# One v buffer, values in a register-addressed PE loop: attention decode on one Trainium2 core

## The chip, the cores and the metric

One core of a Trainium2 chip (trn2). The metric is the device time of one execution in microseconds (us), median of several executions. The engines: PE multiplies matrices, DVE is the vector engine, ACT the scalar engine; SyncE (SP) issues the loads, which sixteen DMA engines carry out. A load has landed when its last part is reported complete. PE's sequencer (`PEq`) is the part of PE that runs the program and hands instructions on.

## The reference

```python
B, H, Sq, Skv, Dh = 8, 32, 1, 4096, 128          # bfloat16
scores = jnp.einsum('bhqd,bhkd->bhqk', q, k) * Dh ** -0.5
attn = jax.nn.softmax(scores, axis=-1)
return jnp.einsum('bhqk,bhkd->bhqd', attn, v)
```

There are 256 heads with one query row each. k and v are 268 MB each and are read once. The kernel takes 8 heads per tile: 32 tiles, each with 8.39 MB of k and 8.39 MB of v.

## The kernel before: the parts that matter

Per tile: DVE multiplies k with the broadcast query row and folds the product (`product`), PE sums over the head dimension by matmuls with the identity (`sum_over_d`), DVE reduces to scores (`scores_of`), ACT takes exponentials (`weights_of`), and one tile later PE multiplies the weights with v (`values_of`). There are two k buffers and **one v buffer**: the next v load can be issued only when PE has read the last one.

```python
KB, VB = 2, 1
...
def load(kind, t):
    ...
        nc.sync.dma_start(buf[:, c0 : c0 + n, :], src[t, :, c0 : c0 + n, :])
...
def values_of(t, lo, hi):                      # 64 matmuls, four column groups
    ...
    for c0 in range(lo, hi, CB):
        i = c0 // CB
        j = group[i]                           # i % 4 for tiles 0 to 30
        nc.tensor.matmul(
            avs[t][j * AG : (j + 1) * AG, :], lhsT=w[:, i, :, :],
            rhs=vt[:, c0 : c0 + CB, :], start=(i < TG), stop=(j not in group[i + 1 :]),
        )
...
for t in range(NT):
    load("k", t + 1); load("v", t)             # (guards cut)
    product(t, 0, Q);  sum_over_d(t, 0)
    if t > 2 and t % R == 1:
        recip_of(n); finish_of(n)              # every eighth tile: writes 16 KB of output
    q_prep(t + 1)
    product(t, Q, 2 * Q);  sum_over_d(t, 1);  scores_of(t, 0)
    values_of(t - 1, 0, C);  copy_of(t - 1)    # (the last two tiles differ)
    product(t, 2 * Q, 3 * Q);  sum_over_d(t, 2);  scores_of(t, 1)
    product(t, 3 * Q, C);  sum_over_d(t, 3);  scores_of(t, 2)
    scores_of(t, 3);  weights_of(t)
    ...
```

## Time and profile before

| | before |
|---|---|
| median (range), us | 1253.25 (1252.86 to 1253.62) |
| span of the profiled run | 1252.0 us |
| data queue (q1), share of sixteen DMA engines | 99.3% = 1243.2 us per engine |
| DVE / PE busy | 1038.0 / 503.5 us |
| v landing to next v issue (mean of 29 tiles) | 6.1 us |

The first three rows say that the loads are the bound. A k load of 19.35 us runs while PE works on v, and the DMA queue's own waits show this (columns: us in total, times, longest):

```profile
SPq L138 <- DMA vt<-in_v_dram: 706.1, 30, 28.0
...
SPq L138 <- PE av L261: 176.2, 29, 10.6
```

For the 29 v loads SyncE waited for PE's values for at most 10.6 us, while DMA engines had a k load to do.

### The profile page before, as it was taken

How to read it: one execution, taken by the hardware profiler on the slowest of the kernel's cores; microseconds unless marked ns; L12 is line 12 of the kernel's file. 1: busy time of each engine (PE TensorE's matmuls, PEld its weight loads, DVE VectorE, ACT ScalarE, POOL GpSimd, SP SyncE). 2: the span in 40 equal slices, each digit the busy share in tenths (PEclk: the TensorE clock that was granted, in tenths of full speed). 3: DMA queues.
4: the chain of work that ended last, by engine and by line, in shares of the span. 5: the costliest groups of instructions: out<-in, count | busy, mean ns of one | idle time of the engine just before them, and what ended most of it. 6: DMA issues, size and time to landing. Idle time of an engine off the chain costs nothing.

```text
span 1252.0 us, 7714 instructions
## 1 busy us (share of the span) xinstructions
PE 503.5 (40%) x3067; PEld 175.8 (14%) x3067; DVE 1038.0 (83%) x588; ACT 172.6 (14%) x625; POOL 3.3 (0%) x18
## 2 busy tenths in 40 slices
PE   1334442444333453334443244432444324445355
PEld 0111110111111111111111111110111101111122
DVE  5988898888988889788898888987879888898991
ACT  0111011111011110111101111011110111101111
POOL 0000000000000000000000000000000000000000
PEclk9766656666556666566665566655666566665767
DMA  9999999999999999999999999999999999999997
GB/s 404 436 434 434 436 434 436 432 436 432 434 437 430 431 432 432 436 432 434 432 432 432 436 436 434 434 425 430 433 430 434 432 432 436 432 430 431 427 448 308
DMA packets 11444, 537.50 MB, mean 429 GB/s; under 512 B 1808, under 2 KB 2064, under 8 KB 2320
## 3 DMA queue, kind: packets, MB, share of 16 engines
q1 hardware_dynamic: 11072, 536.94, 99.3%
q8 instruction: 24, 0.39, 0.1%
q10 hardware_dynamic: 336, 0.07, 0.0%
q14 instruction: 12, 0.10, 0.0%
HBM read 536.94 MB, written 0.07 MB: 429 GB/s over the span
## 4 chain that ended last, share of the span: by engine, by line
DMA 75%; PE 15%; DVE 8%; issue 1%; ACT 0%; SPq 0%
DMA vt<-in_v_dram 74%; PE av L261 14%; DVE kt L171 5%; DVE kt L174 2%; PE ps L191 1%; DMA q_all<-in_q_dram 1%; DVE kt L179 0%; DVE sc L203 0%; DVE pmax L213 0%; SPq L138 0%; DVE spread L215 0%; DVE nmax L220 0%; ACT comb L288 0%; PE op L303 0%; ACT stage L312 0%
## 5 line engine op out<-in xcount | busy, mean ns | idle before, releaser
L171 DVE TENSOR_TENSOR kt<-kt,qb 128x8192 bf16<-128x8192 bf16 x128 | 565.2, 4415 | 92.4 <-DMA kt<-in_k_dram 80.8
L191 PE MATMUL ps<-kt,ident 128*128 128x512 bf16 x792 | 292.2, 527 | 663.5 <-DVE kt L179 508.5
L174 DVE TENSOR_TENSOR kt<-kt 128x4096 bf16<-128x4096 bf16 x128 | 293.4, 2292 | 4.4
L191 PEld LDWEIGHTS <-ident 128*128 128x128 bf16 x792 | 91.9, 119 | 824.7 <-issue 669.3
L261 PE MATMUL av<-vt,w 128*32 128x512 bf16 x2047 | 183.5, 529 | 52.0 <-DMA vt<-in_v_dram 52.0
L233 ACT ACTIVATE w<-sc,bias 128x256 bf16<-128x256 f32 x256 | 126.3, 494 | 357.8 <-DVE bias L224 357.8
L203 DVE TENSOR_REDUCE sc<-ps 128x64 f32<-128x512 f32 x128 | 87.8, 686 | 84.2 <-PE ps L191 84.2
L261 PEld LDWEIGHTS <-w 128*32 128x32 bf16 x2047 | 67.8, 127 | 178.9 <-issue 86.8
L288 ACT ACTIVATE comb<-av 128x512 bf16<-128x512 f32 x32 | 19.1, 596 | 424.7 <-PE av L261 424.7
L179 DVE TENSOR_TENSOR kt<-kt 128x2048 bf16<-128x2048 bf16 x58 | 71.0, 1225 | 2.0
L233 ACT ACTIVATION_READ_ACCUMULATOR w<-sc,bias 128x1 f32 x256 | 47.7, 186 | 0.0
L154 ACT ACTIVATE qg<-qh 8x128 bf16<-8x128 f32 x32 | 8.6, 267 | 186.9 <-PE qh L150 186.9
L312 ACT ACTIVATE stage<-op,rz 16x128 bf16<-16x128 f32 x16 | 5.7, 358 | 96.0 <-DVE rz L281 72.9
L303 PE MATMUL op<-comb,pick 128*16 128x128 bf16 x128 | 15.9, 265 | 4.6 <-ACT comb L288 4.6
L213 DVE TENSOR_REDUCE pmax<-sc 128x1 f32<-128x256 f32 x32 | 13.4, 420 | 1.1
L150 PE MATMUL qh<-q_all,ident 128*8 128x128 bf16 x32 | 8.5, 267 | 13.2 <-DMA q_all<-in_q_dram 13.2
L281 DVE RECIPROCAL rz<-zp 16x1 f32<-16x1 f32 x16 | 2.4, 148 | 13.3 <-PE zp L273 13.3
L156 PE MATMUL qp<-qg,heads 8*128 8x128 bf16 x32 | 8.3, 259 | 12.7 <-ACT qg L154 12.7
L303 PEld LDWEIGHTS <-pick 128*16 128x16 bf16 x128 | 9.0, 102 | 15.9 <-issue 15.8
L158 ACT ACTIVATE qb<-qp 128x128 bf16<-128x128 f32 x32 | 8.9, 278 | 11.1 <-PE qp L156 11.1
L215 DVE TENSOR_SCALAR spread<-same,pmax 128x32 f32<-128x32 f32 x32 | 7.7, 242 | 1.1
L224 DVE TENSOR_SCALAR bias<-own,nmax 128x8 f32<-128x8 f32 x32 | 7.4, 231 | 1.1
(25 smaller groups left out, 24.3 us busy)
## 6 DMA issues: line engine op xcount, KB each, us to landing
kt<-in_k_dram SPq DMA_DIRECT2D x7, 4096.0 KB, 35.3
kt<-in_k_dram SPq DMA_DIRECT2D x2, 2048.0 KB, 36.4
vt<-in_v_dram SPq DMA_DIRECT2D x1, 4096.0 KB, 40.7
vt<-in_v_dram SPq DMA_DIRECT2D x1, 2048.0 KB, 45.2
vt<-in_v_dram SPq DMA_DIRECT2D x1, 1024.0 KB, 47.2
vt<-in_v_dram SPq DMA_DIRECT2D x1, 512.0 KB, 48.0
vt<-in_v_dram SPq DMA_DIRECT2D x31, 32.9
kt<-in_k_dram SPq DMA_DIRECT2D x28, 43.7
```

Of the source, the lines that this page charges most:

```text
L154: nc.scalar.activation(out=qg[:], in_=qh[:], func=ACT.Copy)
L158: nc.scalar.activation(out=qb[:, 0, :], in_=qp[:], func=ACT.Copy)
L171: nc.vector.tensor_tensor(out=part, in0=part, in1=qb[:].to_broadcast([P, MC, D]), op=ALU.mult)
L174: nc.vector.tensor_tensor(out=part[:, :, 0 : D // 2], in0=part[:, :, 0 : D // 2], in1=part[:, :, D // 2 : D], op=ALU.add,)
L179: nc.vector.tensor_tensor(out=part[:, :, 0 : D // 4], in0=part[:, :, 0 : D // 4], in1=part[:, :, D // 4 : D // 2], op=ALU.add,)
L191: nc.tensor.matmul(ps[:], lhsT=ident[:], rhs=kt[:, u * UC : (u + 1) * UC, s * DS : (s + 1) * DS], start=(s == 0), stop=(s == n - 1),)
L203: nc.vector.tensor_reduce(out=scs[t][:, u * UC : (u + 1) * UC], in_=sums.pop((t, u))[:], axis=AX.X, op=ALU.add)
L213: nc.vector.tensor_reduce(out=pmax[:], in_=sc[:], axis=AX.X, op=ALU.max)
L233: nc.scalar.activation(out=w[:, :, g, :], in_=sc_g, func=ACT.Exp, bias=bias[:, g : g + 1], scale=scale, accum_out=esum[:, t % R, g : g + 1],)
L261: nc.tensor.matmul(avs[t][j * AG : (j + 1) * AG, :], lhsT=w[:, i, :, :], rhs=vt[:, c0 : c0 + CB, :], start=(i < TG), stop=(j not in group[ ...
L288: nc.scalar.activation(out=comb[:], in_=av, func=ACT.Copy)
L303: nc.tensor.matmul(ops[n][:], lhsT=pick[:, m, r, :], rhs=comb[:, m, :], start=(r == 0 and m == 0), stop=(r == R - 1 and m == CB - 1),)
```

## The change

The intent is to shorten PE's program (a loop in place of 64 unrolled matmuls per tile) and to keep DVE from waiting for PE, by putting the last two score quarters behind the next tile's first product. The loop's matmuls take their operands' addresses from registers, and all 64 matmuls of a tile go into one column group of PE (32 of its 128 columns) in place of four. `tc.tile_critical()` makes a region of the loop. Cut to its core:

```diff
-    sc_pool = ... bufs=1
+    sc_pool = ... bufs=2
+def values_loop(t):
+    ...
+    av = avs[t][0:AG, :]                       # one column group
+    with tc.tile_critical() as loop:
+        for i in range(EDGE): one(i, start=(i == 0), stop=False)        # EDGE = 2
+        end = (NV - EDGE) * nw
+        pe.reg_mov(rw, EDGE * nw); pe.reg_mov(rv, EDGE * nv)
+        with pe.While(lambda: pe.snap(rw, ...) < end):
+            ow = pe.snap(rw, ...); ov = pe.snap(rv, ...)
+            for i in range(LOOP):                                       # LOOP = 6
+                pe.matmul(av, lhsT=wf[:, bass.ds(ow + i * nw, nw)],
+                          rhs=vf[:, bass.ds(ov + i * nv, nv)], start=False, stop=False)
+            pe.reg_add(rw, rw, LOOP * nw); pe.reg_add(rv, rv, LOOP * nv)
+        for i in range(NV - EDGE, NV): one(i, start=False, stop=(i == NV - 1))
@@ order of a tile with a loop (0 < t <= NT - 3)
+            q_prep(t + 1)
             product(t, 0, Q)
             sum_over_d(t, 0)
+            scores_of(t - 1, 2); scores_of(t - 1, 3); weights_of(t - 1)
             if t > 2 and t % R == 1: recip_of(n); finish_of(n)
             product(t, Q, 2 * Q)
             sum_over_d(t, 1)
             scores_of(t, 0)
-            values_of(t - 1, 0, C)
+            values_loop(t - 1)
+            load("k", t + 1); load("v", t)     # were at the top of the tile
             copy_of(t - 1)
```

## The prediction

> **What bounds the kernel now.** I read, in this order, the page's slices, its table of DMA queues, the chain that ended last, the waits of the DMA queue, and a timeline of one tile in the middle.
>
> ```profile
> DMA  9999999999999999999999999999999999999997
> GB/s 404 436 434 434 436 434 436 432 436 432 434 437 430 431 432 432 436 432 434 432 432 432 436 436 434 434 425 430 433 430 434 432 432 436 432 430 431 427 448 308
> ...
> q1 hardware_dynamic: 11072, 536.94, 99.3%
> q8 instruction: 24, 0.39, 0.1%
> ...
> L191 PE MATMUL ps<-kt,ident 128*128 128x512 bf16 x792 | 292.2, 527 | 663.5 <-DVE kt L179 508.5
> ...
> L261 PE MATMUL av<-vt,w 128*32 128x512 bf16 x2047 | 183.5, 529 | 52.0 <-DMA vt<-in_v_dram 52.0
> ```
>
> The data queue holds the sixteen DMA engines for 99.3% of 1252.0 us, which is 1243.3 us per engine. The first packet starts at 1.76 us and the last one ends at 1246.8 us by the packet records, so nothing is left between; 5.2 us of tail follow. DVE is busy 1038.0 us, 32.4 per tile, and PE 503.5 us, 15.7 per tile: neither binds. The load of one tile (8.39 MB of k or of v) takes 8.39 MB / 434 GB/s = 19.35 us, the pair 38.7 us, and 32 pairs are 1238 us. This is the bound, and no work on PE makes it shorter. The skill's page "DMA: Bandwidth & Descriptors", section "Where 436 GB/s comes from", works out 435.2 GB/s as the ceiling of the sixteen ports; the slices lie at 430 to 437.
>
> The timeline of one tile, cut to what matters, shows what this hangs on:
>
> ```profile
> 67.89 4.23 PE L261 MATMUL av<-vt,w 128*32 128x512 bf16 x64
> ...
> 606.44 6.29 PE L261 MATMUL av<-vt,w 128*32 128x512 bf16 x64 [1.41 <-DMA vt<-in_v_dram]
> ...
> 612.78 0.33 SPq L138 DMA_DIRECT2D vt<-in_v_dram  x1
> ...
> 620.34 0.33 SPq L138 DMA_DIRECT2D kt<-in_k_dram  x1
> ...
> 625.85 4.42 DVE L171 TENSOR_TENSOR kt<-kt,qb 128x8192 bf16<-128x8192 bf16 x1 [3.56 <-DMA kt<-in_k_dram]
> ```
>
> There is one v buffer. A v tile lands at 606.4; PE multiplies it in 6.29 us; only then is the next v issued (612.78), while the k tile of that gap runs until 625.8. So the values may last longer at no cost until the v issue comes too late for the end of the k load. The k issue at 620.34 has the whole v load ahead of it and is far from late.
>
> **What the Trainium skill says.** "TensorE: Matmul & The Clock Gate", section "Wait — 56ns, not 53.3ns?", gives start to start 426.7 ns for 512 columns while the array is cold and 215.7 once warm; its Part 1 has a cold start last about 3.4 us of sustained work, in free-running windows. The trace agrees: four matmuls of four column groups start together, the next four 427 ns later, or 216 ns later once warm; the 64 take 4.23 to 6.5 us depending on when the clock rises (16 x 0.216 = 3.5 if all were warm). "TensorEngine Tiling", section "Available Configurations", has four independent tiles of 128x32; the 183.5 us of L261 over 2047 matmuls are 90 ns each, so they do run four abreast. "Advanced Engine Details and Errata", section "Control Flow Timing": an unconditional branch about 51 ns, compare-and-branch about 108. No run here has shown a loop yet. The warm bursts in this trace issue four weight loads and matmuls per 216 ns, so a fixed-address pair costs the sequencer 54 ns at most; for register addresses neither a page nor the trace has a cost.
>
> **The change, part by part.**
> *Values in one column group.* The 64 matmuls of tiles 0 to 28 (29 tiles) go one after another. Cold they cost 0.427 us each, warm 0.216. Before, the cold part lasted (from 16 x 0.216 + 0.211 n = 5.15 to 6.5, n = 8 to 14 groups) some 3.4 to 6 us. Now the loop follows the sums of the second quarter almost without a gap, so part of that is spent before it: I take 4 us. 4 / 0.427 = 9 cold ones, then 55 x 0.216 = 11.9: about 15.9 us, from 15.2 to 17. This adds 10 us of PE time per tile: (15.9 - 5.73) x 29 = 295 us of busy time, to some 800 us, and it lies beside the loads if the window holds it.
>
> *The loop's sequencer work.* Ten rounds of six matmuls, with two fixed ones at each end. In the built program each looped matmul has one fused register instruction ahead of it, each round one more, a register move, a compare-and-branch and a branch. My estimate from the skill's figures: 159 ns of branches per round; for the eight register instructions I assume 60 ns each, as for the slow decode of a matmul (about 62 ns, the same section of the clock gate page): 480; the six pairs with register addresses at twice 62 if they leave the fast path: 744. Sum 1383 ns per round, 231 per matmul; at 54 ns per pair it would be 161. Against 216 in the array the first is just about equal, and the cold start gives the sequencer a lead. So the array sets the 15.9 us, unless the register instructions cost much more than assumed. This is the step that I know least.
>
> *The window.* A v tile's data end about 0.5 us before its landing (last packet about 605.9, landing 606.4), and the first packet starts 1.0 us after the issue (0.74 to 1.76 at the start of the kernel). After a v landing the k load runs 19.35 us, so the issue may come 19.35 - 0.5 - 1.0 = 17.8 us after the landing. From this goes the entry. DVE starts tile t at its k landing; two quarters took 15.84 us (625.85 to 641.69), now with the two late score reductions and the four small steps between them (2.4 us): 18.3. The sums of the second quarter follow (4 x 0.427 = 1.8 and the latency of 0.2), so PE is free at 20.3, about 1.0 us after the v landing at 19.25. The waits and the branch into the loop I put at 0.4, the drain and the semaphore at its end at 0.25. Left for the loop: 17.8 - 1.0 - 0.4 - 0.25 = 16.1 us. The mean loop fits with 0.2 to spare, a cold one misses by up to 0.9. With lengths evenly between 15.2 and 17 the mean overrun is 0.2 us, 29 x 0.2 = 6 us on the path. A late v shifts all that follows, but the next entry then waits less for the sums.
>
> *Scores behind the next product.* DVE does the same work in another order (128 reductions of 0.68 us). This keeps DVE from waiting for sums of quarters 2 and 3, which PE now does after the loop, at about 37 us into the tile; DVE wants them at 38.7 + 8. Weights come at 10.5 + 4.0 (eight exponentials of 0.49) = 14.5 us into the next tile, 4.8 before the v landing. Hidden.
>
> *Fewer instruction fetches.* PE's rows fall from 6088 to 3014. The 24 fetches of 16 KB hold an engine 1.06 us each;[...] the completion records show the slowest of the sixteen 5 us behind the fastest at the end. Some nine fetches fewer are 9 x 1.06 / 16 = 0.6 us on average, on the slowest engine perhaps 1 to 1.5. Gain about 1.5.
>
> Sum: 1253.25 + 6 - 1.5 = 1257.8.
>
> **The rivals.**
> *The loop fits wholly.* If the sequencer is quick and the clock rises early, only the fetches count: 1251 to 1252. For it: 16 us is near the mean loop; the change looks sized for the window.
> *The sequencer binds.* At 300 ns per matmul the loop is 9 x 0.427 of lead and then the sequencer: 64 x 0.3 = 19.2 less what was fetched ahead, about 18.8 us. Then the v loads set the period: 19.35 + 1.5 + 0.65 + 18.8 = 40.3 instead of 38.7, 29 x 1.6 = 46 us: 1300. At 350 ns (21.8 us) the period is 43.3 and the time 1386. Nothing in the trace speaks against it.
> *The clock stays low* with a quarter of the array's columns at work: 64 x 0.427 = 27.3 us, period 48.8, 29 x 10.1 = 293 us: about 1545. Against it:[...] unlikely.
> *A gain over 2%* would need the bytes to move faster than 434 GB/s; the packets of 64 KB take 2.42 us each throughout. I see no way.
>
> **Range and chances.** The central number is 1258, barely over what the loads need. Low is 1247, if the spread between the engines vanishes. High is 1345, which holds the sequencer at some 325 ns per matmul. The chance that the loop exceeds the window by more than 0.86 us per tile (25 us, 2%) I put at 0.37, from not knowing the cost of register addresses; within 2% 0.62; faster 0.01.
>
> **What would show it.** In the profile after: the time from the first to the last values matmul of a tile (15 to 17 us), the step between two of them (216 ns warm; more says the sequencer); the v issue at most 17.8 us after the v landing; the DMA slices still at 9 and 430 GB/s. Wrong if the slices fall to 8 and the DMA queue waits for PE's sequencer while no load is running, or if the values run at 427 ns throughout; the fetch step is right if instruction packets on PE's queue drop to about 15.

## The result, and the profile after

After: 1332.78 us median (1325.84 to 1339.63, 4 runs) against 1253.24 (1252.86 to 1253.62, 4 runs) in the same rounds: ratio 1.0635, 95% interval 1.0578 to 1.0691, slower by 6.4%. A ratio here is the mean time of one kernel's fast runs over that of the other's fast runs of the same rounds, so it is not quite the ratio of the medians quoted. All outputs are right. The time lies in the predicted range; the likeliest class predicted, within 2%, was wrong, and so was the central number (5 us of loss predicted, 79.5 measured).

From the page of the kernel after (`x` counts instructions; the two figures behind the bar are us in sum and mean ns):

```profile
span 1332.6 us, 11055 instructions
...
DMA  9999999999988999999999799999999989999998
GB/s 411 441 378 428 405 425 408 382 429 388 441 379 347 411 407 437 386 403 380 411 425 420 321 409 414 435 411 410 409 412 439 410 342 410 411 414 404 389 402 347
...
q1 hardware_dynamic: 11072, 536.94, 94.8%
q8 instruction: 14, 0.23, 0.1%
...
L290 PE MATMUL av<-vt,w 128*32 x1740 | 432.9, 408 | 2.1
```

The same bytes now move in 80.6 us more (1332.6 less 1252.0). The queue's own line splits this: 94.8% of 1332.6 us is 1263.3 us of work per engine, 20 more than before, so packets took longer; and 69.3 us per engine are idle instead of 8.8, so 60.5 more. Most slices have lost a little, and three have dips to 347, 321 and 342 (the 347 at the very end is the tail). (`L290` means 408 ns because durations of overlapping matmuls are summed; the start-to-start step is what counts, below.)

The DMA queue's waits after:

```profile
SPq L154 <- DMA vt<-in_v_dram: 565.3, 30, 20.7
SPq L154 <- PEq L280: 532.6, 29, 24.0
```

For 29 v loads SyncE now waits for PE's loop, up to 24.0 us each. One tile of the timeline (start, us, engine, line):

```profile
580.65 0.33 SPq L154 DMA_DIRECT2D vt<-in_v_dram  x1
...
582.39 4.42 DVE L188 TENSOR_TENSOR kt<-kt,qb 128x8192 bf16<-128x8192 bf16 x1 [9.62 <-DMA kt<-in_k_dram]
...
600.80 1.87 PE L209 MATMUL ps<-kt,ident 128*128 128x512 bf16 x4 [8.49 <-DVE kt L197]
...
606.49 1.03 PE L276 MATMUL av<-vt,w 128*32 128x512 bf16 x2 [3.82 <-DVE kt L188]
...
607.32 15.35 PE L290 MATMUL av<-vt,w 128*32 x60
...
622.72 0.60 PE L276 MATMUL av<-vt,w 128*32 128x512 bf16 x2
...
623.49 0.33 SPq L154 DMA_DIRECT2D vt<-in_v_dram  x1
...
624.98 4.43 DVE L188 TENSOR_TENSOR kt<-kt,qb 128x8192 bf16<-128x8192 bf16 x1 [9.71 <-DMA kt<-in_k_dram]
```

By the completion records this v landed at 605.38. PE starts 1.1 us later, is done some 16.8 us after that, and v is issued at 623.49. The k load that covers the gap has landed in full at 624.88, so v was issued 1.4 us before. What the DMA engines do around that issue is in the table of stretches (us, busy time and count of each engine, clock, DMA share, GB/s), first of the kernel after:

```profile
core 0: us, PE busy (x) PEld busy (x) DVE busy (x) ACT busy (x) POOL busy (x), PEclk, DMA share, GB/s
612.00:618.00 6.00, 6.00 (x29) 2.49 (x26) 3.23 (x2) 0.00 (x0) 0.00 (x0) 1.00 0.86 371
618.00:624.00 6.00, 5.60 (x24) 2.08 (x24) 0.00 (x0) 0.45 (x1) 0.00 (x0) 1.00 0.43 186
624.00:630.00 6.00, 3.93 (x23) 1.79 (x22) 4.99 (x2) 0.68 (x3) 0.00 (x0) 1.00 1.00 382
```

and the same clock time of the kernel before, whose v issue is at 612.78:

```profile
612.00:618.00 6.00, 2.88 (x26) 1.11 (x19) 5.97 (x3) 0.60 (x1) 0.00 (x0) 1.00 1.03 448
618.00:624.00 6.00, 2.83 (x12) 0.91 (x9) 2.02 (x6) 1.63 (x7) 0.00 (x0) 0.56 0.96 415
624.00:630.00 6.00, 0.00 (x0) 0.10 (x1) 4.16 (x1) 2.41 (x10) 0.00 (x0) 0.50 1.06 459
```

In the six microseconds before 624 the engines of the kernel after are busy for 0.43 of the time, although a load is running until 624.88 and the next is issued at 623.49. (A share over 1 is a packet counted where it began.) In the stretch behind it they are all busy at 382 GB/s; the three stretches of the kernel before average 441. So the first packets are slow.

**Reading the packets.** The records do not name the engine of a packet, but per load they hold 128 packets of 64 KB and 16 of 4 bytes: eight for each of the sixteen engines, and then one of 4 bytes. I took the sixteen ends of each k load (the 4-byte packets) and the sixteen first packets of the v load behind it, matched in order of time, for 28 v loads of each of seven kernels (before, after, and e1, e2, e3, e5, e6 below): 3136 pairs. The 335 whose issue came later than in the first row are left out.

| v issued before the engine's own end of k, us | pairs | idle gap, median us | first packet, median us |
|---|---|---|---|
| -0.5 to 0 (after it) | 251 | 1.32 | 3.12 |
| 0 to 0.5 | 282 | 0.88 | 3.12 |
| 0.5 to 1 | 281 | 0.45 | 3.06 |
| 1 to 1.5 | 234 | 0.45 | 2.93 |
| 1.5 to 2 | 176 | 0.02 (mean 0.27) | 2.57 |
| 2 to 2.5 | 166 | 0.01 | 2.42 |
| over 2.5 | 1411 | 0.01 | 2.42 |

An engine that has run dry starts 1.05 us after the issue, and its first packet takes 3.1 us instead of 2.42. An engine that still has work needs the next load some 2 to 2.5 us before its end to lose next to nothing. And the sixteen engines do not end together: in the kernel after the first one ends a k load 1.9 us before the last (mean), in the kernel before 3.3 us. So the issue has to come some 4 to 5 us before the last data of the running load. (The expectations below have 3.5; the run with 42 zero matmuls, e11, still loses 0.2 us per tile at a mean of 4.2.) In the kernel after it comes 0.74 us before the last engine's end and 1.16 us *after* the first one's.

**Three dips.** At tiles 8, 16 and 24 PE waited for something else (columns as above):

```profile
PE av L276 <- PEq L280: 50.5, 13, 9.8
...
PE av L276 <- DMA out_dram<-stage: 24.8, 3, 8.5
```

The program has the write of finished output (issued by ACT) ahead of the loop, and the loop's region waits at its entry for that transfer. The timeline of the first of the three:

```profile
385.61 0.39 ACTq L377 DMA_DIRECT2D out_dram<-stage  x1
...
399.40 1.04 PE L276 MATMUL av<-vt,w 128*32 128x512 bf16 x2 [8.26 <-DMA out_dram<-stage]
```

This write of 16 KB took 13.2 us to land while the loads ran (issued 385.61, landed 398.83). v had landed at 393.19, and with the usual 1.1 us PE would have started at 394.3: 5.1 us lost. With 5.9 and 6.5 at the other two it is 17.5 us.

### The profile page after: what moved, and what is told of

Read it like the earlier page. It is cut to its first block, busy times and chain, and to the rows that moved or that the text cites. A ratio compares the mean times of both kernels' runs of the same rounds, so it can differ in the third digit from the quotient of the medians.

```text
span 1332.6 us, 11055 instructions
## 1 busy us (share of the span) xinstructions
PE 762.6 (57%) x3067; PEld 293.1 (22%) x3067; DVE 1035.4 (78%) x588; ACT 170.8 (13%) x625; POOL 3.3 (0%) x18
## 3 DMA queue, kind: packets, MB, share of 16 engines
q1 hardware_dynamic: 11072, 536.94, 94.8%
## 5 line engine op out<-in xcount | busy, mean ns | idle before, releaser
L209 PE MATMUL ps<-kt,ident 128*128 128x512 bf16 x792 | 250.4, 472 | 431.2 <-DVE kt L197 379.1
L290 PE MATMUL av<-vt,w 128*32 x1740 | 432.9, 408 | 2.1
L290 PEld LDWEIGHTS av<-vt,w 128*32 x1740 | 178.7, 103 | 262.2 <-issue 109.3
L209 PEld LDWEIGHTS <-ident 128*128 128x128 bf16 x792 | 86.0, 111 | 582.7 <-issue 532.3
L346 ACT ACTIVATE comb<-av 32x512 bf16<-32x512 f32 (+1 forms) x32 | 18.7, 586 | 757.2 <-PEq L280 749.8
L276 PE MATMUL av<-vt,w 128*32 128x512 bf16 x116 | 47.5, 502 | 103.9 <-PEq L280 50.5
L276 PEld LDWEIGHTS av<-vt,w 128*32 128x32 bf16 x116 | 7.6, 101 | 142.2 <-issue 140.3
L318 PE MATMUL av<-vt,w 128*32 128x512 bf16 x191 | 15.5, 423 | 0.7 <-DMA vt<-in_v_dram 0.6
L362 PE MATMUL op<-comb,pick 32*16 32x128 bf16 (+1 forms) x128 | 12.3, 215 | 4.8 <-ACT comb L346 4.8
L167 PE MATMUL qh<-q_all,ident 128*8 128x128 bf16 x32 | 7.2, 225 | 13.2 <-DMA q_all<-in_q_dram 13.2
L362 PEld LDWEIGHTS <-pick 32*16 32x16 bf16 (+1 forms) x128 | 6.8, 84 | 12.0 <-issue 11.6
L318 PEld LDWEIGHTS <-w 128*32 128x32 bf16 x191 | 6.6, 105 | 9.4 <-issue 5.2
## 6 DMA issues: line engine op xcount, KB each, us to landing
kt<-in_k_dram SPq DMA_DIRECT2D x2, 2048.0 KB, 25.6
```

The costliest lines, as they stand in the source:

```text
L209: nc.tensor.matmul(ps[:], lhsT=ident[:], rhs=kt[:, u * UC : (u + 1) * UC, s * DS : (s + 1) * DS], start=(s == 0), stop=(s == n - 1),)
L276: pe.matmul(av, lhsT=wf[:, i * nw : (i + 1) * nw], rhs=vf[:, i * nv : (i + 1) * nv], **how)
L290: pe.matmul(av, lhsT=wf[:, bass.ds(ow + i * nw, nw)], rhs=vf[:, bass.ds(ov + i * nv, nv)], start=False, stop=False,)
L318: nc.tensor.matmul(avs[t][j * AG : (j + 1) * AG, :], lhsT=w[:, i, :, :], rhs=vt[:, c0 : c0 + CB, :], start=(i < TG), stop=(j not in group[ ...
L346: nc.scalar.activation(out=comb[0:n, :, :], in_=av[0:n, :, :], func=ACT.Copy)
L362: nc.tensor.matmul(ops[n][:], lhsT=pick[0:e, m, r, :], rhs=comb[0:e, m, :], start=(r == 0 and m == 0), stop=(r == R - 1 and m == CB - 1),)
```

## The experiments

The theory after the first look: v's issue comes too late for the DMA queue, which costs some 2.3 us in each of 29 tiles, and the three waits for the output cost 17 us. The rivals: the loop itself (its sequencer or its registers), the lower rate of a busier PE, or the new order of the scores.

**e1: the new order alone.** Fixed addresses, four column groups, all else as in the change:

```diff
-        with tc.tile_critical() as loop: ...
+        for i in range(NV):
+            j = i % TG
+            pe.matmul(avs[t][j * AG : (j + 1) * AG, :], ..., start=(i < TG), stop=(i >= NV - TG))
```

> The late scores alone, values with fixed addresses in four column groups. My theory (the v issue comes too late for the end of the k load, and a DMA queue that runs dry costs more than the gap): v is issued some 7 us after its predecessor landed, far inside the window, so the time is that of the kernel before, 1251 to 1256 us. Rival (the new order of scores itself delays DVE or the release of k buffers): clearly slower, 1270 us or more.

Measured: 1253.41 us, ratio 0.9999 (0.9982 to 1.0015). The values start 1.0 us after the v landing, and v is issued 6.1 us after it. The order of the scores and the moved loads cost nothing.

**e2: one column group, unrolled.** The change with its loop and region taken out:

```diff
-        with tc.tile_critical() as loop: ...
+        for i in range(NV):
+            one(i, start=(i == 0), stop=(i == NV - 1))
```

> All of the change but the loop: one column group and late scores, fixed addresses, no registers, no critical region. My theory: the entry of 1.1 us falls to 0.05 and the ten steps of 0.2 us between rounds go, so v is issued about 16.3 us after a landing instead of 17.75, near the edge of the window: 1253 to 1285 us. Rival (one column group alone makes the values too long, the loop costs nothing): 1315 to 1335 us, as the whole change without the waits for the output.

Measured: 1272.82 us (1272.21 to 1273.30), ratio 1.0152 (1.0135 to 1.0169). v is issued 16.2 us after the landing, and already 19.5 us are lost, without any loop.

```profile
span 1271.5 us, 7719 instructions
...
q1 hardware_dynamic: 11072, 536.94, 98.8%
```

98.8% of 1271.5 is 1256.2 us of work per engine, 13.0 more than before, and 15.3 us idle, 6.5 more. So a third of the loss is idle engines and two thirds are slow packets. This alone refutes the prediction's edge of 17.8 us. The entry that I expected at 0.05 us is 0.8 in the mean: here the sums of the second quarter end about 1.0 us after the landing (median), and the values start behind them.

**e3: the output behind the loop.** The change, with `recip_of` and `finish_of` moved:

```diff
-            if t > 2 and t % R == 1:
+            if t > 2 and t % R == 1 and not loop:
                 recip_of(n); finish_of(n)
...
                 copy_of(t - 1)
+                if t > 2 and t % R == 1:
+                    recip_of(n); finish_of(n)
```

> The whole change, but the reciprocal, the scaling and the write of results come after the loop of their tile. My theory: in three tiles the entry into the loop waits for the write of 16 KB to land (6 to 7.6 us after the v landing instead of 1.1); with the write behind the loop this goes and the time falls by about 17 us, to 1315. Rival (these three entries are late for another reason, or the time is lost elsewhere then): within 5 us of 1332.

Measured: 1315.85 us (1309.40 to 1321.93), ratio 1.0513 (1.0473 to 1.0554): 16.9 us less than the change. The runs of both kernels scatter over 12 to 14 us, and by the two intervals the difference is known to some 9 us; the 17.5 us read at the three tiles agree with it. The wait for `out_dram` is gone from PE's waits, and the three dips from the slices:

```profile
GB/s 419 419 397 424 421 419 391 417 413 417 419 387 418 417 417 421 411 419 416 413 423 415 420 413 387 449 387 416 417 391 443 415 389 418 415 417 409 383 430 321
```

**e4 and e7: twenty matmuls per round,** without and with e3's edit. At 60 = 3 x 20 there are two round boundaries in place of nine inside the loop.

```diff
-LOOP = 6
+LOOP = 20
```

> The whole change with three rounds of 20 matmuls instead of ten of 6. Every boundary between rounds costs 0.2 us, so the values end 7 x 0.2 = 1.4 us earlier and v is issued 16.3 us after the landing. My theory (dry queue): more than the 1.4 us per tile comes back, since the queue no longer runs dry: at least 29 x 1.4 = 41 us, up to 60: 1272 to 1292 us. Rival (each late microsecond costs just one, and the rest is the loop's own overhead elsewhere): 41 us, 1292. Rival (the sequencer binds): no change or slower.

> Late output and three rounds of 20 together. In the run with three rounds the waits for the output grew (the three entries came 6 to 11 us late, 28 us in sum), which hid part of what the shorter loop gave. My theory: with both, v is issued 16.3 to 17 us after the landing and no entry waits for the output: 1317 - 28 = 1289, so 1282 to 1296 us. Rival (the boundaries cost nothing on the path): 1310 to 1320, as with late output alone.

Measured: e4 1317.29 us, ratio 1.0519 (1.0479 to 1.0559), a miss; e7 1288.55 us, ratio 1.0288 (1.0273 to 1.0304), a hit. The boundary stalls vanish, and the issue comes 17.2 us (e4, without the three output tiles) and 17.0 us (e7) after the landing, 0.6 to 0.8 earlier than in the change. What e4's expectation left out is that the three waits for the output can grow: PE started 10.3, 11.1 and 4.2 us later than the usual 1.1 at those tiles, 25.6 in sum instead of 17.5 (e7's expectation has 28, from a first reading). Why they grew was not taken apart. The edit of e3 is worth 28.7 us here and 16.9 there; with the scatter of these runs it is barely shown that the two effects do not simply add.

**e5, e6, e11, e12: lateness alone.** e1 with zero-weight matmuls that read v added before the last four, no loop, no region, no change of the result:

```diff
+        for _ in range(PAD):                   # 36 in e5, 54 in e6, 42 in e11, 48 in e12
+            pe.matmul(avs[t][0:AG, :], lhsT=w_zero[:], rhs=vf[:, 0:nv], start=False, stop=False)
```

> No loop at all: the late scores alone (values with fixed addresses in four groups), plus 36 matmuls with zero weights in one column group that read the v tile before it is released (36 x 0.216 = 7.8 us; the result stays right). v is issued 6.1 + 7.8 = 13.9 us after a landing, 4.9 us before the k data end. My theory (the queue needs some 3.5 us of lead and then loses nothing): 1252 to 1257 us, though PE works 250 us more. Rival (the busier PE, or its higher clock, costs time by itself): 1270 or more.

> The same with 54 zero matmuls: v is issued some 17.5 us after its predecessor landed, as late as in the changed kernel, but without registers, critical region or loop. My theory (only the lateness of the issue counts): as the changed kernel without its waits for the output, 1300 to 1320 us. Rival (the loop itself, its branches or waits on the other engines make the loss, and an issue 17.8 us after the landing is in time, as I predicted): 1253 to 1260 us.

> The late scores alone with 42 zero matmuls added. My theory: each of the sixteen DMA engines needs the next v load issued about 2 us before it ends its own part of the running k load, and the first engine ends 2 to 3 us before the last. From the runs with 36 and 54 zero matmuls the issue should come 14.9 us after the v landing, some 1.5 to 2 us before the first engine ends: about 0.2 us lost per tile, 1255 to 1263 us. Rival (the prediction's own window: only the end of the load less 1.0 us counts, 17.8 us after the landing): no loss, 1253 to 1257 us, as with 36.

> The same with 48 zero matmuls: the issue about 16.0 us after the v landing, about 1 us before the first engine ends its part and 3 us before the last one does. My theory: like the unrolled kernel in one column group, whose issue came 16.2 us after the landing: 0.5 to 0.7 us lost per tile in idle time and slow first packets, 1266 to 1276 us. Rival (17.8 us is the edge): no loss, 1253 to 1258 us.

Measured: 36: 1256.33 us, ratio 1.0033 (1.0018 to 1.0049). 42: 1265.23 us (1262.57 to 1269.59), 1.0096 (1.0071 to 1.0122). 48: 1273.78 us, 1.0165 (1.0145 to 1.0184). 54: 1294.02 us, 1.0328 (1.0296 to 1.0359). e12 is a hit; e6 lies 6 us under its range, and e11 2 us over its own (its profiled run took 1263.0 us, the edge of the range). The loss grows with the lateness, from almost nothing at 13.8 us to 40 us at 17.1, and it starts well before 17.8. All these kernels run with fixed addresses, so neither the loop nor its region is needed for it; and with 36 the values take 12.4 us from first to last start in place of 4.7, which costs 3 us in all, so a busier PE is not the cause either (busy 655.7 us there; and 731.5 in e10 below, which loses 3 us too). The page of the run with 54:

```profile
span 1290.5 us, 10852 instructions
...
q1 hardware_dynamic: 11072, 536.94, 97.6%
```

97.6% of 1290.5 us are 1259.5 us of work per engine, 16 more than before, and 31.0 us idle, 22 more: slow packets and idle engines, as in the change.

**The account.** For each kernel, the mean over engines and over the same 28 loads of the idle gap plus the excess of the first packet over 2.42 us, times 29, against the gain in span over 1252.0 us:

| kernel | v issue after landing | before the first / last engine's end | loss per tile | x 29 | span gained |
|---|---|---|---|---|---|
| e1 | 6.1 us | 9.67 / 12.91 us | 0.00 us | 0 | -0.3 us |
| e5, 36 zero matmuls | 13.8 | 2.49 / 5.24 | 0.09 | 2.5 | 1.8 |
| e11, 42 | 14.9 | 1.95 / 4.20 | 0.23 | 6.5 | 9.2 |
| e12, 48 | 16.1 | 1.04 / 3.15 | 0.67 | 19.4 | 20.9 |
| e2, unrolled | 16.2 | 1.10 / 3.12 | 0.63 | 18.3 | 19.5 |
| e7 | 17.0 | 0.41 / 2.23 | 1.21 | 35.1 | 34.4 |
| e6, 54 | 17.1 | 0.29 / 2.37 | 1.24 | 36.0 | 38.5 |
| e3 | 17.8 | -0.35 / 1.40 | 1.89 | 54.8 | 55.6 |
| e4 | 18.1 | -0.58 / 1.26 | 2.14 | 62.2 | 64.9 |
| after | 18.4 | -1.16 / 0.74 | 2.73 | 79.2 | 80.6 |

Idle engines and slow first packets account for the whole loss to within 4 us in every row, whatever made the issue late. (The means of e4 and after include the three output waits; without these tiles the issue comes 17.2 and 17.8 us after the landing. In the first three rows of the table the packets were put together engine by engine, since matching in order of time alone gives e1 a negative loss. e3's profiled run is the shortest of its four, 6 us under their median.)

**e8, e9, e10: v in two halves.** If lateness is the cause, a v buffer in two halves, each freed when half of the values are done, should hide the loop. e8 puts k's load and the first half's load between two loops of 32 values; e9 puts both loops ahead of the loads; e10 is e9 with fixed addresses. All three have e3's edit.

```diff
-    buf = pool.tile([P, C, D], BF16, name=f"{kind}t", tag=home)
+    half = pool.tile([P, C // 2, D], BF16, name="vt", tag=f"v{h}")   # h = 0, 1
...
-                values_loop(t - 1)
-                load("k", t + 1); load("v", t)
+                values_loop(t - 1, 0)
+                load("k", t + 1); load("v", t, (0,))  # e8; in e9 and e10 both halves
+                values_loop(t - 1, 1)                 # e8; in e9 and e10 ahead of the loads
+                load("v", t, (1,))                    # e8
```

> The loop in two halves, each with its own half of the v buffer and its own load, late output, four rounds of 7 in each. The first half is released some 10 us after the landing, the second 19 us after it, but that one is wanted 9.7 us later. My theory: both issues have more than 3.5 us of lead, nothing is lost, and fewer instruction fetches remain: 1250 to 1254 us. Rival (the loop costs time by itself, on queues or other engines): 1280 or more.

> The loop in two halves again, but both loops now stand ahead of the k load in the program. In e8 the second loop began only when the k load that stood before it had landed (28 waits, 224 us), as a critical region waits for every DMA that stands ahead of it. My theory: with that mended the halves are released about 10 and 19 us after the landing, both early enough for the queue (the second is wanted 9.7 us later), and nothing is lost: 1250 to 1255 us. Rival (the loop costs time by other ways as well, by its branches on all engines or its two entries): 1270 or more.

> The same with fixed addresses in place of the two loops: 24 instruction fetches on PE's queue instead of some 17. If fewer fetches are worth what I predicted (1.5 us for ten fewer), this is about 1 us above the split loop; if they are worth nothing, the two are equal within 1 us. By my theory of the lead this one too lies at 1251 to 1255 us.

e8: 1346.69 us, ratio 1.0739 (1.0721 to 1.0758), a miss, and worse than the change. PE's waits give the reason:

```profile
PE av L287 <- DMA kt<-in_k_dram: 223.7, 28, 9.6
```

The second region waits at its entry for the k load that I had put ahead of it in the program, 8.0 us in each of 28 tiles. It is the output wait of the change again, made worse; e9 moves that load behind both regions, and there the wait is gone from PE's list.

e9: 1261.02 us (1260.54 to 1262.14), ratio 1.0059 (1.0046 to 1.0073). e10: 1256.48 us (1255.83 to 1257.57), ratio 1.0026 (1.0012 to 1.0039). The loop in halves is thus hidden in the steady part: at 1150 us both had moved the same 496.0 MB (before: 497.0). I had expected e9 at 1250 to 1255 and e10 a little above it, at most 1255; both lie over their ranges, and it is the other way round. The loss of e9 lies in the last tiles. Its timeline:

```profile
1152.93 1.03 PE L287 MATMUL av<-vt,w 128*32 128x512 bf16 x2 [3.61 <-DMA vt<-in_v_dram]
...
1177.07 4.42 DVE L196 TENSOR_TENSOR kt<-kt,qb 128x8192 bf16<-128x8192 bf16 x1
...
1208.50 3.64 PE L335 MATMUL av<-vt,w 128*32 128x512 bf16 x64
...
1210.46 2.05 SPq L155 DMA_DIRECT2D vt<-in_v_dram  x2
```

and that of e10:

```profile
1145.86 13.99 PE L287 MATMUL av<-vt,w 128*32 128x512 bf16 x64
...
1165.29 4.42 DVE L196 TENSOR_TENSOR kt<-kt,qb 128x8192 bf16<-128x8192 bf16 x1
...
1196.73 3.64 PE L317 MATMUL av<-vt,w 128*32 128x512 bf16 x64
...
1198.68 2.05 SPq L155 DMA_DIRECT2D vt<-in_v_dram  x2
```

In e9 the region of the first half waits until the second half has landed too (1152.4), so the last loops end 11.5 us later than e10's matmuls; the sums of the last quarter stand behind them, DVE starts tile 30 12 us later, and the v load of tile 30 is issued at 1210.46, 0.2 us before the last k data land (1210.70). There the queue runs dry once more. e9's last data land 2.8 us after e10's, and its tail behind them is 3 us longer, together the 6 us between the two spans. What is left of e10 over before, 2.4 us of span, is about what 62 half loads cost by an estimate: one takes 9.71 us, 0.04 more than half of 19.35, and 62 x 0.04 is 2.5 us; no run isolates it. No version beat the kernel before. A loop that keeps four column groups was not tried.

## Why the prediction was right or wrong

**The range: met by luck.** Its upper part, up to 1345, was there for a sequencer at some 325 ns per matmul. The loop ran as predicted, and the time came into the range by the two steps below that were wrong or missing. The sign of being wrong that the prediction had named did show: four slices of the steady part at 8 or 7, and SyncE waiting for PE's sequencer (532.6 us in 29 waits) while DMA engines stand idle.

**The bound: right.** The loads carry the time, and what PE does matters only through the v issue. (Of the slices read as 430 to 437, three inner ones lie outside: 425, 427 and 448.)

**Loop length and clock: right.** First to last start is 16.04 us in the mean (15.75 to 16.54) against 15.9 predicted; steps are 427 ns cold (4 of them in the tile at 895.6 us, 11 in that at 936.7), then 216 but for the round boundaries of the next paragraph. The rival in which the clock stays low is out.

**Sequencer: nearly right.** Once the lead of the cold start is used up, a round of six takes 1506 ns (one step of 421, one of 221, four of 216), 251 ns per matmul against my 231 (the register instructions that I assumed at 60 ns take 74 in this trace). A round of seven in e9 takes 1659. From the two, an estimate: 153 ns per register-addressed pair and 588 per round. So the sequencer does pace the end of a loop that warmed early, but a loop that warmed late has it hidden, and the sum stays at 16. The rival of 1300 us (300 ns per matmul) comes near the result for a reason that does not hold: e6 and e12 lose time with no register address at all.

**Entry: right in sum, by two errors.** I had 1.0 us for late sums and 0.4 for waits and branch. The values start 1.14 us after the landing (median); but since the loads slip, the sums are done before v lands, mostly by 1 to 2 us, and the whole 1.1 us goes to the entry of the region.

**Issue time: right.** Entry, loop and end put the v issue at 17.55 us after the landing by my terms; 17.7 was measured, without the first tile and the three with output waits (18.4 over all 29).

**The window: the step that failed.** "The issue may come 19.35 - 0.5 - 1.0 = 17.8 us after the landing." The 1.0 us from issue to first packet is right (1.05). But I set it against the end of the *last* engine's packets, as if one end counted. The first of sixteen engines ends about 2 us earlier; it runs dry, starts late, and its first packet takes 0.7 us more. And an engine needs the issue 2 us before its end, not 1.0. The real edge is therefore 14 to 15 us after the landing (e5 loses under 0.1 us per tile at 13.8, e11 0.2 at 14.9), not 17.8. The term "mean overrun 0.2 us, 29 x 0.2 = 6 us" should have been about 2 us per tile: e3, which has lateness alone, loses 1.9 per tile. I had even noted that the slowest engine ends 5 us behind the fastest, and used it only for the instruction fetches.

**The output waits: missing.** The region waits at its entry for transfers ahead of it in the program (the output here, a k load in e8), and I did not ask which transfers those are. It is worth 16.9 us by e3, known to some 9 us. The 62.5 us that e3 still loses are lateness: of the 55.6 us in its profiled run, the account above finds 54.8.

**Fewer fetches: right in number, not seen in time.** The instruction packets of queue q8 fell from 24 to 14. e9 and e10 were to show their worth and did not, since e9 loses its time elsewhere. The 1.5 us stay open.

**Scores behind the next product: right.** Free by e1.

**Open:** why a first packet after idle time takes 3.1 us, and why an engine needs 2 us of lead where an idle one starts in 1.05. The records show both, and no run here takes them apart.

## What to carry to other kernels

With one buffer between a load and its reader, ask not whether the reader ends before the queue is empty, but whether the next load is issued before the *first* DMA engine is out of work, with 2 us or more to spare: here 4 to 5 us before the last data. Look at the lead in every tile of the trace before stretching anything that stands ahead of an issue; of the 11.6 us by which the issue moved here the first 8 were nearly free, and the last 4 cost 2 us per tile. And when work goes into a region that waits for what precedes it, list the transfers ahead of it in the program: move what need not be there behind it.

## What the Trainium skill lacked or had wrong

- "DMA: Bandwidth & Descriptors" gives the ceiling of 435.2 GB/s (section "Where 436 GB/s comes from"), and the trace agrees (434 over one load), but not what it takes to stay there from one load to the next: an engine needs the next load about 2 us before its end, and the first 64 KB packet of one that ran dry takes 3.1 us in place of 2.42. For the start of a transfer issued like these the page has about 0.6 us (first-byte latency of HWDGE, section "Latency and other measured facts"); here 1.05 us pass from the start of the issuing instruction, which itself takes 0.33 us, to the first packet. Where its section "Anatomy of one DMA — SWDGE (gpsimd) path" lays the fixed 2 us of a transfer mostly on completion (its path is another one), for these loads, issued by SyncE, the start is the larger part: 1.05 us from issue to first packet, against a median of 0.35 (after) to 0.47 us (before) from the last packet to the landing.
- No page was found to say how far apart the sixteen engines end one load: 1.9 us in the kernel after, 3.3 in the kernel before.
- "Advanced Engine Details and Errata", section "Control Flow Timing", has 51 and 108 ns for branches. A loop round of six register-addressed matmuls took 1506 ns, of which an estimate from two round sizes lays 588 ns on the round and 153 on each pair; the page has nothing on register-addressed operands.
